# Three early quads of a fused attention and SiLU kernel take an M2 tile in 64-row halves

## The chip, the cores and the metric

The kernel runs on one core of a Trainium2 chip. The core has a matrix engine (TensorE, PE in the profile, whose weight loads are listed apart as PEld), three engines for elementwise work (VectorE or DVE, ScalarE or ACT, GpSimd or POOL), a queue engine (SyncE or SP) and 16 DMA engines. The metric is the device time of one execution in microseconds (us); lower is better.

## The reference

Per batch and head: scores, a causal mask with a decay from the cumulative sum of log f, softmax, times V. The result, laid out as 4608 tokens by 512, goes through two matrix products with a SiLU between them.

```
scores = scale * q @ k^T + (cum[i] - cum[j]),  -1e9 above the diagonal   # B=8, H=8, S=576, D=64
attn   = softmax(scores) ;  x = (attn @ v) as [4608, 512]
h = x @ w_in            # [512, 2048]
g = h * sigmoid(h)
out = g @ w_out         # [2048, 512]
```

## The kernel before

**Attention.** The decay is folded into V: V is multiplied by exp(-cum) on POOL (`convert_v`, L420), a column of ones in V gives the softmax denominator, and no maximum is subtracted. The first 128 query rows of all batches are done ahead of the main loop (the functions whose names end in 0). The main loop treats the other 448 rows. Heads go in pairs `n` (32 of them, four for each batch); two pairs are one *quad* `m` (16 of them). For a pair, `scores(n, c)` with c = 0, 1, 2 runs the score matmuls in three chunks (L470). Their contraction is over 64, so they are given to one half of the array's rows each ("64*128" in the profile), the two heads of a pair on the two halves at once. ACT takes the exponential (L481, and L475 for the 64 last rows). `mask` and `mask_tail` (L487, L493, DVE) clear what lies above the diagonal. `attend(n)` (L517, L526) multiplies with V on the full array, and DVE divides by the denominator (L534, L535) into `xr`. `back(m)` turns the quad's `xr` into columns of x: by seven PE transposes and two DVE copies (L559, L562, L565) for m = 0, 1, 2 and 15, by two DMA transposes on SP (L549, L553) for the others (`BY_DMA`).

**The two products.** x is held in 13 groups of 512, 384 or 256 tokens. *M1* is x @ w_in: `m1_chunk(g, fc)` makes one of 16 chunks of a group with four full-array matmuls (L578), a tanh on ACT (L586) and one DVE operation that completes twice the SiLU into `gt` (L587). *M2* is g @ w_out: a tile of 128 tokens is 16 full-array matmuls over 512 columns (L623), issued in four parts, and an ACT copy with the factor 0.5 (L633). A second form of M2, `m2_rows` (L640), does a tile with 64 matmuls over 64 rows and 256 columns (L649), two at a time on the two halves of the array, in two halves of 32 matmuls; it writes two PSUM tiles `pr` in place of one `po`. Between its halves DVE reads one column (`m2_fence`, L660), and `m2_out` (L662) evicts with two DVE operations (L666). PSUM is split in two score buffers (`psc`) and four others (`pbig`), which `hp`, `po`, `pr`, `tx` and `dn` share.

**What sets the order.** All five engines run in the order in which the program is written; nothing is reordered. `wanted` (L690) says whether M1 or M2 is next, `step` issues one chunk or part, `fill` and `slot` issue as many as fit in a number of microseconds at the planned rate, and `rest` goes on until the quad has its share (`QUAD`, L929). `whole` (L914) finishes an M2 tile that has been begun and a group whose M1 has at most four chunks left; it returns the next M2 tile, or nothing if there is none that may be started. `store` (L599) puts output DMAs on SP. `turn(n)` (L889) issues the work for later pairs: the cast of pair n+3 on POOL, the loads of pair n+4 on SP and POOL, a batch's V loads and conversions, and the DMA transpose of pair n+3 on SP (L438).

**The main loop** (L961) has two forms of a quad. Quads 0 to 3, without rows, run three bursts of scores with M1 and M2 between them on the full array: burst, `back`, slot, burst, slot, burst, slot, both `attend`, slot. Quads 4 to 15 start with `whole`, and if it gives a tile they run burst, first half of the M2 tile in 64-row form, burst, second half, burst, and put M1 and M2 chunks behind the first and the second `attend`. Here are the lines that choose:

```
rows = whole() if m > 0 and BY_DMA[m - 1] else None
scores(n, 0)
scores(n, 1)
if m > 0:
    back(m - 1)
```

Of the kernel before, what the change touches and what calls it, by code (L numbers as in the profile page):

```python
# [18 lines left out]
def kernel(  # L19
# [130 lines left out]
    def head(p, i):  # L150
        return p // 2 * 4 + 2 * i + p % 2
# [347 lines left out]
    BY_DMA = [3 <= m < NQ - 1 for m in range(NQ)]  # L499

    def attend(n):
        b, p = divmod(n, NP)
        if p % 2 == 0:
            xqs[n // 2] = xqp.tile([P, NGR, 2, D], BF16, name="xr", tag="xr", bufs=3)
        xq = xqs[n // 2]
        u, ut = us.pop(n), uts[n % 4]
        dn = pbig.tile([P, NGR, D + 1], FP32, name="dn", tag="big")

        def vals(kb, i):
            h = head(p, i)  # L510
            return v0[b][:, h, :] if kb == 0 else vbf[b][:, kb - 1, h, :]

        for i in range(2):
            for c in range(1, NM):
                for kb in range(c + 1):
                    o = AT[c, kb]
                    nc.tensor.matmul(  # L517
                        dn[:, i * NR + c - 1, :],
                        lhsT=u[:, i, o : o + P],
                        rhs=vals(kb, i),  # L520
                        start=(kb == 0),
                        stop=(kb == c),
                    )
        for i in range(2):
            for kb in range(NM + 1):
                nc.tensor.matmul(  # L526
                    dn[:, NGR - 1, :],
                    lhsT=ut[:, kb, i : i + 2, :].rearrange("p i t -> p (i t)"),
                    rhs=vals(kb, i),
                    start=(i == 0 and kb == 0),  # L530
                    stop=(i == 1 and kb == NM),
                )
        rec = recp.tile([P, NGR], FP32, name="rec", tag="rec")
        nc.vector.reciprocal(out=rec[:, :], in_=dn[:, :, D])  # L534
        nc.vector.tensor_tensor(  # L535
            out=xq[:, :, p % 2, :],
            in0=dn[:, :, 0:D],
            in1=rec[:, :, None].to_broadcast([P, NGR, D]),
            op=ALU.mult,
        )  # L540
# [58 lines left out]
    def store(n):  # L599
        n = max(n, 0)  # L600
        for q_, dst, src in stores[:n]:
            q_.dma_start(out=dst, in_=src)
        del stores[:n]
# [79 lines left out]
    at = {"m1": 0, "m2": 0, "left": 0.0}  # L683
# [23 lines left out]
    def step(force=0):  # L707

        a, c = at["m1"], at["m2"]
        want = wanted(a, c)  # L710
        if not want:
            return None
        g1 = M1[a][0] if a < len(M1) else NG
        g2 = M2[c][0] if c < len(M2) else NG
        can1 = g1 in ready and not (M1[a][1] == 0 and g1 > g2 + lag["g"])
        can2 = open2["w"] and c < len(M2) and g2 < g1
        kind = force if (force == 1 and can1) or (force == 2 and can2) else want
        if kind == 1:
            if M1[a][1] == 0:
                begin[g1] = (0, c)  # L720
            m1_chunk(g1, M1[a][1])
            at["m1"] += 1
            t = 4 * (GW[g1] / 2.4 + 2.5)
        else:
            m2_part(*M2[c])
            at["m2"] += 1
            t = 4 * (DM / 2.4 + 2.5)
        return t

    def behind():  # L730
        t = sum(4 * (GW[g] / 2.4 + 2.5) for g, _ in M1[at["m1"] :] if g in ready)
        t += sum(4 * (DM / 2.4 + 2.5) for g, _, _ in M2[at["m2"] :] if g in ready)
        return t / 1000
# [180 lines left out]
    def whole():  # L914

        while at["m2"] < len(M2) and M2[at["m2"]][2] and wanted(at["m1"], at["m2"]):
            t = step(2)
            at["left"] -= t / 1000
        c = at["m2"]
        while M1[at["m1"]][0] in ready and M1[at["m1"]][1] >= NFC - 4 and M2[c][0] == M1[at["m1"]][0]:  # L920
            at["left"] -= step(1) / 1000
        a = at["m1"]
        if c >= len(M2) or M2[c][2]:
            return None
        g1 = M1[a][0] if a < len(M1) else NG
        return M2[c][:2] if M2[c][0] < g1 else None

    LAG, LOW = 13.0, 2.0
    QUAD = [10.9] * (NQ // 2) + [11.7] * (NQ // 2)  # L929

    def spent():
        t = sum(4 * (GW[g] / 2.4 + 2.5) for g, _ in M1[: at["m1"]])
        return (t + at["m2"] * 4 * (DM / 2.4 + 2.5)) / 1000
# [15 lines left out]
    def passed():  # L949
        for x in pending:  # L950
            x[0] -= 1
        while pending and pending[0][0] == 0:
            ready.update(pending.pop(0)[1])

    def slot(us_, least=0, ends=(0, 0)):
        n = len(stores)
        fill(us_, least, ends)
        store(n)
        passed()

    for m in range(NQ):  # L961
        n = 2 * m
        piece = 1.7 if m < 2 else 2.4
        if m == 2:
            assert at["m2"] >= M2_OF[0]
            first_pool.__exit__(None, None, None)
            gpools[0] = ctx.enter_context(tc.tile_pool(name="third", bufs=1))
            lag["g"] = 2
        if m == 4:
            lag["parts"] = 12  # L970
        goal = (spent() if m <= 4 else goal) + QUAD[m]
        rows = whole() if m > 0 and BY_DMA[m - 1] else None
        scores(n, 0)
        scores(n, 1)
        if m > 0:
            back(m - 1)
        turn(n)
        if m > 0:
            if m % 2 == 0:
                b = m // 2 - 1  # L980
                pending.append([2, [REST_OF[b]] + ([TAILS_OF[b][0]] if b == NM - 1 else [])])
        if rows:
            at["m2"] += 4
            m2_rows(*rows, 0)
            m2_fence(*rows)
            mask(n)
            scores(n, 2)
            scores(n + 1, 0)
            turn(n + 1)
            m2_rows(*rows, 1)  # L990
            mask_tail(n)
            mask(n + 1)
            scores(n + 1, 1)
            scores(n + 1, 2)
            m2_out(*rows)
            passed()
            attend(n)
            mask_tail(n + 1)
            slot(1.9, 3)
            attend(n + 1)  # L1000
            slot(1.8)
            rest(goal)
            at["left"] = 0.0
            continue
        slot(piece, 0, (1, 0))
        mask(n)
        scores(n, 2)
        scores(n + 1, 0)
        turn(n + 1)
        slot(piece, 0, (1, 0))  # L1010
        mask_tail(n)
        mask(n + 1)
        scores(n + 1, 1)
        scores(n + 1, 2)
        mask_tail(n + 1)
        slot(piece, 0, (1, 0))
        attend(n)
        attend(n + 1)
        slot(min(3.5, max(0.8, behind() - LAG)) if m > 1 else 0.8)
# [40 lines left out]
```

## Time and profile before

| what | value |
|---|---|
| time, median of 3 runs | 340.76 us (340.21 to 341.42) |
| the profiled execution | 340.02 us, of which the span is 338.2 us |
| PE busy | 328.6 us, 97% |
| ACT, DVE, POOL busy | 216.7, 191.4, 157.8 us |
| M1 matmuls (L578) | 122.5 us in 700 records |
| M2 matmuls (L623, L649) | 89.8 us and 46.0 us |
| score matmuls (L470) | 27.8 us and more for the part against `kT` |

The profile shows one execution. Each line of a timeline starts with the start time and the duration in us; "x8" says that eight instructions are merged, and a bracket gives the idle time before them and what ended it. Matmuls overlap, so the step from the start of one group to the start of the next is the time that PE spent on it. A few matmul records are missing, so a group can show x3 where four ran. Times of a quad below run from its first score matmul to that of the next.

### The profile page before, as it was taken

What the parts mean: (1) busy time and instruction counts of PE and PEld (TensorE: products, weight loads), DVE (VectorE), ACT (ScalarE), POOL (GpSimd) and SP (SyncE); (2) the same over time, 40 slices, a digit from 0 to 9 for tenths busy, and PEclk for the clock granted to TensorE, in tenths of its full rate; (3) what the DMA queues carried; (4) which work ended last, traced back from release to release, by engine and by line L of the source; (5) the groups of instructions that cost most, each with busy time, mean ns of one, the idle gap of its engine ahead of it and who ended that gap; (6) DMA issues with size and microseconds to landing.
All of it is one profiled execution on the core that took longest, in us unless ns stands there. A gap on an engine that the chain in (4) does not pass through costs nothing.

```text
span 338.2 us, 9998 instructions
## 1 busy us (share of the span) xinstructions
PE 328.6 (97%) x4101; PEld 222.4 (66%) x4132; DVE 191.4 (57%) x425; ACT 216.7 (64%) x389; POOL 157.8 (47%) x241
## 2 busy tenths in 40 slices
PE   8999999999999999999999999999999999999995
PEld 3745655577656767858767796867777685555654
DVE  4667736276567456655655865785485565334330
ACT  5757645776777676848748794875778583444431
POOL 8895417637885675493493656819060000000000
PEclk9999999999999999999999999999999999999998
DMA  8999999999999999999999979969673200101012
GB/s 152 196 196 220 167 200 168 200 238 171 183 227 176 136 189 147 187 185 155 168 181 144 175 126 194 186 104 184 119 129 64 60 33 20 44 33 64 31 64 62
DMA packets 124542, 48.00 MB, mean 142 GB/s; under 512 B 111824, under 2 KB 118224, under 8 KB 124496
## 3 DMA queue, kind: packets, MB, share of 16 engines
q1 hardware_dynamic: 93200, 31.10, 51.1%
q0 software_dynamic: 31136, 16.13, 37.1%
q8 instruction: 32, 0.52, 0.7%
q10 hardware_dynamic: 160, 0.13, 0.1%
q14 instruction: 14, 0.11, 0.1%
HBM read 36.85 MB, written 9.44 MB: 137 GB/s over the span
## 4 chain that ended last, share of the span: by engine, by line
PE 87%; DMA 6%; POOL 3%; issue 1%; ACT 1%; DVE 0%; POOLq 0%
PE hp L578 33%; PE po L623 24%; PE pr L649 12%; PE sc L470 7%; PE dn L517 6%; DMA vf<-in_v_dram 5%; PE dn L526 3%; DMA qkb<-in_k_dram 1%; POOL v L350 1%; PE tp L295 1%; POOL qkb L132 1%; PE tx L559 1%; POOL w_in_bf L200 0%; ACT u L481 0%; ACT osb L633 0%
## 5 line engine op out<-in xcount | busy, mean ns | idle before, releaser
L587 DVE SCALAR_TENSOR_TENSOR gt<-th,hp 128x384 bf16<-128x384 bf16 (+2 forms) x208 | 107.2, 523 | 71.1 <-ACT th L586 62.7
L586 ACT ACTIVATE th<-hp 128x384 bf16<-128x384 f32 (+2 forms) x208 | 96.6, 471 | 73.8 <-PE hp L578 71.9
L578 PE MATMUL hp<-x,w_in_bf 128*128 128x384 bf16 (+2 forms) x700 | 122.5, 321 | 0.4
L578 PEld LDWEIGHTS <-w_in_bf 128*128 128x128 bf16 x832 | 78.9, 98 | 48.9 <-issue 0.5
L623 PE MATMUL po<-w_out_bf,gt 128*128 128x512 bf16 (+1 forms) x374 | 89.8, 370 | 1.7 <-issue 0.6
L481 ACT ACTIVATE u<-sc 128x1024 bf16<-128x1024 f32 (+1 forms) x96 | 74.7, 819 | 7.0 <-PE sc L470 7.0
L623 PEld LDWEIGHTS <-gt 128*128 128x128 bf16 x400 | 37.6, 98 | 32.5 <-issue 0.2
L411 POOL CAST qkb<-qf 128x384 bf16<-128x384 f32 x32 | 16.6, 520 | 74.6 <-DMA qf<-in_q_dram 74.0
L649 PE MATMUL pr<-w_out_bf,gt 64*128 64x256 bf16 x768 | 46.0, 269 | 0.0
L158 POOL DMA_DIRECT2D qkb<-in_k_dram x56 | 43.7, 782 | 0.6 <-issue 0.6
L649 PEld LDWEIGHTS <-gt 64*128 64x128 bf16 x768 | 38.6, 94 | 2.8
L424 POOL TENSOR_TENSOR vp<-vf,w_bf 128x520 bf16<-128x520 f32 (+1 forms) x32 | 34.3, 1075 | 9.2 <-DMA vf<-in_v_dram 7.5
L633 ACT ACTIVATE osb<-po 128x512 f32<-128x512 f32 (+1 forms) x25 | 14.6, 584 | 26.4 <-PE po L623 26.4
L470 PE MATMUL sc<-qkT 64*128 64x128 bf16 (+1 forms) x640 | 27.8, 206 | 0.3 <-ACT u L481 0.3
L487 DVE TENSOR_TENSOR u<-u,tri 128x768 bf16<-128x768 bf16 x32 | 20.6, 645 | 10.5 <-ACT u L481 10.5
L470 PEld LDWEIGHTS <-qkT 64*128 64x128 bf16 x640 | 20.0, 94 | 8.2 <-issue 6.5
L475 ACT ACTIVATE ut<-sc 128x640 bf16<-128x640 f32 x32 | 22.7, 709 | 1.9 <-PE sc L470 1.7
L517 PEld LDWEIGHTS <-u 128*128 128x128 bf16 x576 | 20.7, 98 | 3.4 <-issue 0.5
L517 PE MATMUL dn<-vp,u 128*128 128x65 bf16 x384 | 22.0, 194 | 0.4 <-issue 0.4
L535 DVE TENSOR_TENSOR xr<-dn,rec 128x448 bf16<-128x448 f32 x32 | 20.0, 624 | 1.1
L189 POOL DMA_DIRECT2D vf<-in_v_dram x24 | 20.2, 859 | 0.0
L517 PE MATMUL dn<-v,u 128*128 128x65 bf16 x192 | 20.0, 194 | 0.0
(73 smaller groups left out, 243.3 us busy)
## 6 DMA issues: line engine op xcount, KB each, us to landing
out_dram<-osb SPq DMA_DIRECT2D x32, 256.0 KB, 3.2
vf<-in_v_dram POOLq DMA_DIRECT2D x24, 256.0 KB, 6.1
qf<-in_q_dram SPq DMA_DIRECT2D x64, 96.0 KB, 3.6
qkb<-in_k_dram POOLq DMA_DIRECT2D x56, 48.0 KB, 3.9
vf<-in_v_dram SPq DMA_DIRECT2D x8, 256.0 KB, 5.3
w_in_bf<-in_moe_w_in_dram POOLq DMA_DIRECT2D x4, 512.0 KB, 7.1
w_out_bf<-in_moe_w_out_dram POOLq DMA_DIRECT2D x4, 512.0 KB, 9.2
qkb<-in_q_dram POOLq DMA_DIRECT2D x8, 128.0 KB, 5.4
```

The lines of the kernel that those rows point to most:

```text
L158: nc.gpsimd.dma_start(out=t2[:, NR + 1 : NX, j * D : (j + 1) * D], in_=k[b, head(p, j), P:SM, :].rearrange("(c p) d -> p c d", p=P),)
L424: nc.gpsimd.tensor_tensor(out=vbf[b][r, c, :, :], in0=vst[b][c][r, :, :], in1=w_bf[r, c + 1, b * H : (b + 1) * H, None].to_broadcast([n, H ...
L470: nc.tensor.matmul(sc[:, i, o : o + q1 - q0], lhsT=kt, rhs=t[r, q0:q1], start=True, stop=True)
L475: nc.scalar.activation(out=ut[:, :, 0:3:2, :].rearrange("p k i t -> p i k t"), in_=sc[:, :, T0 : T0 + (NM + 1) * ST].rearrange("p i (k t) ...
L481: nc.scalar.activation(out=u[:, :, c * SM : c * SM + w], in_=sc[:, :, 0:w], func=ACT.Exp, scale=scale)
L487: nc.vector.tensor_tensor(out=x, in0=x, in1=tri[:, None, None, :].to_broadcast([P, 2, NR, P]), op=ALU.mult)
L517: nc.tensor.matmul(dn[:, i * NR + c - 1, :], lhsT=u[:, i, o : o + P], rhs=vals(kb, i), start=(kb == 0), stop=(kb == c),)
L578: nc.tensor.matmul(hp[:, :], lhsT=w_in_bf[:, cc, fc * P : (fc + 1) * P], rhs=xcols(g, cc), start=(cc == 0), stop=(cc == NCC - 1),)
L586: nc.scalar.activation(out=th[:, :], in_=hp[:, :], func=ACT.Tanh, scale=0.5)
L587: nc.vector.scalar_tensor_tensor(out=gt[:, fc, :], in0=th[:, :], scalar=1.0, in1=hp[:, :], op0=ALU.add, op1=ALU.mult,)
L623: nc.tensor.matmul(po[:, :], lhsT=gt[:, fc, tb * P : (tb + 1) * P], rhs=w_out_bf[:, fc, m0:m1], start=(fc == 0), stop=(fc == NFC - 1),)
L649: nc.tensor.matmul(pos[g, tb][y], lhsT=gt[r, fc, tb * P : (tb + 1) * P], rhs=w_out_bf[r, fc, y * DM // 2 : (y + 1) * DM // 2], start=(half ...
```

## The change

`whole` is now called ahead of every quad, so a quad of the first four takes the 64-row form too if there is a tile to start. A new function `ones(k)` issues k chunks of M1. In the first four quads all stores that are due are issued at the head of the quad. Where `back(m - 1)` is made by PE transposes in a quad with rows, it moves behind the three score bursts and the first `attend` (`late`).

```
+    def ones(k):
+        n = len(stores)
+        for _ in range(k):
+            step(1)
+        at["left"] = 0.0
+        store(n)
+        passed()
...
-        rows = whole() if m > 0 and BY_DMA[m - 1] else None
+        rows = whole()
+        late = bool(rows) and m > 0 and not BY_DMA[m - 1]
+        if m < 4:
+            store(len(stores))
         scores(n, 0)
         scores(n, 1)
-        if m > 0:
+        if m > 0 and not late:
             back(m - 1)
         turn(n)
...
             attend(n)
             mask_tail(n + 1)
-            slot(1.9, 3)
+            if late:
+                back(m - 1)
+            if m < 2:
+                ones(4)
+            else:
+                slot(1.9, 3)
             attend(n + 1)
+            if m < 4:
+                if m < 2:
+                    ones(2)
+                else:
+                    slot(min(5.3, max(0.8, behind() - LAG)))
+                continue
             slot(1.8)
             rest(goal)
```

The order that comes out, M1 and M2 chunks by quad (a unit is one chunk of M1 or one part of M2; g is the group, tb the tile):

| quad | before | after |
|---|---|---|
| 0 | M2 g1 tb0 parts 0-2, M1 g2 chunks 0-5, among the bursts | M2 g1 tb0 whole, in rows; M1 g2 chunks 0-3, then 4-5 |
| 1 | M2 g1 tb0 part 3, tb1 parts 0-2; M1 g2 chunks 6-12 | M2 g1 tb1 whole, in rows; M1 g2 chunks 6-9, then 10-11 |
| 2 | M2 g1 tb1 part 3, g2 tb0, g2 tb1 part 0; M1 g2 chunks 13-15, g3 chunks 0-5 | M1 g2 chunks 12-15 first; M2 g2 tb0 whole, in rows; M2 g2 tb1 parts 0-2; M1 g3 chunks 0-4 |
| 3 | M2 g2 tb1 parts 1-3; M1 g3 chunks 6-13 | M2 g2 tb1 part 3 first; no rows, as no M2 tile may be started; M1 g3 chunks 5-6, 7-10, 11-14 between the bursts and 15 at the end |
| 4 | M1 g3 chunks 14-15 first; rows from here on | rows from here on |

The whole work is the same. PE has 64 matmuls in place of 16 for three M2 tiles, ACT three copies fewer, DVE six evictions and three fences more. From quad 4 on the two orders differ by one or two units. In the changed kernel an M2 part stands right ahead of the first scores of quads 14 and 15, as it does in quads 5, 7 and 9 of both.

## The prediction

> **What bounds the kernel now.** I read the page first, then who waited for the score matmuls, then PE's timeline through two kinds of quad, then the busy time in stretches cut at the quads.
>
> ```profile
> span 338.2 us, 9998 instructions
> ...
> PE 87%; DMA 6%; POOL 3%; issue 1%; ACT 1%; DVE 0%; POOLq 0%
> ```
>
> PE is 87% of the chain that ended last, so a change is worth what it takes from PE's own time or from PE's waits. A view of the score line says what ended PE's idle time ahead of it:
>
> ```profile
>   issue: 7.6, 24
>   ACT u L481: 0.3, 1
> ```
>
> 24 gaps end in "issue": the engine waited for nothing recorded. 24 is also 3 bursts in each of quads 0 to 3 and one in each of the other 12: the places where full-array work gives way to 64-row work. PE's timeline, here in quad 2 and quad 4, gives their price:
>
> ```profile
> 83.73 1.04 PE L578 MATMUL hp<-x,w_in_bf 128*128 128x256 bf16 x8
> 84.70 0.23 PE L470 MATMUL sc<-qkT 64*128 64x128 bf16 x2
> ...
> 109.92 1.91 PE L649 MATMUL pr<-w_out_bf,gt 64*128 64x256 bf16 x32
> 111.67 0.22 PE L470 MATMUL sc<-qkT 64*128 64x128 bf16 x2
> ```
>
> M1 runs at 0.437 us a chunk of 256 columns (four matmuls of 0.109, the step between chunks that follow one another), 0.650 a chunk of 384; an M2 part takes 0.863. Two chunks need 0.87 from 83.73, to 84.60; scores start at 84.70. A crossing costs 0.10, and the way back the same. A half tile in rows takes 111.67 - 109.92 = 1.75, with no gap on either side; two are 3.50 against 3.45 for the four parts.
>
> In stretches cut at the quads' first scores (columns: length, then busy time and instructions of PE, PEld, DVE, ACT, POOL, then clock and DMA):
>
> ```profile
> 61.94:71.33 9.39, 8.92 (x140) 6.29 (x142) 4.66 (x13) 7.52 (x14) 6.93 (x11) 1.00 1.17 245
> 71.33:81.92 10.59, 10.33 (x153) 7.38 (x156) 7.68 (x20) 8.44 (x18) 6.23 (x9) 1.00 1.47 173
> 81.92:96.36 14.44, 14.34 (x170) 8.89 (x173) 7.68 (x19) 9.68 (x18) 11.89 (x16) 1.00 1.15 174
> 96.36:109.47 13.11, 12.95 (x164) 8.11 (x165) 8.78 (x21) 10.48 (x19) 8.61 (x13) 1.00 1.27 218
> 109.47:123.64 14.17, 14.06 (x207) 10.13 (x209) 7.96 (x19) 9.06 (x15) 10.82 (x17) 1.00 1.01 172
> 137.62:152.46 14.84, 14.74 (x211) 10.51 (x213) 8.51 (x20) 9.55 (x16) 10.38 (x15) 1.00 1.30 193
> 152.46:165.21 12.75, 12.73 (x207) 9.76 (x206) 8.25 (x20) 10.05 (x17) 7.02 (x11) 1.00 1.40 174
> ```
>
> These are quads 0 to 4, 6 and 7. The clock is full throughout. I take M1 and M2 at the rates above off each length; what remains is attention, crossings and waits. Quad 0: 3 parts and 6 chunks are 5.21, rest 4.18. Quad 1: 6.51, rest 4.08. Quad 2: 10.39, rest 4.05. Quad 3 with the two chunks ahead of quad 4: 9.09, rest 4.02. Quads 4, 6 and 7 in rows: 10.80, 11.45 and 9.30, rest 3.37, 3.39 and 3.45. ACT has most of the rest of a quad: 10.48 of 13.11 in quad 3.
>
> **The change, part by part.** I sum against the profiled execution, 340.02 us (span 338.2 and 1.8 around it); the median, 340.76, stands 0.74 above it.
>
> *Quads 0 to 2 go to rows.* Crossings: three bursts with two each become one with two, so 4 x 0.105 = 0.42 a quad less, and 0.05 more for the slower tile. The quads show less than that, since scores in rows come closer to ACT: quads 4, 6 and 7 rest at 3.40 on average without `back`, and the seven transposes of `back` step 0.39 on PE (82.47 to 82.87 with its gap, 0.40). A quad with rows and late transposes is thus 3.79. Quad 1: 4.08 to 3.79, -0.29. Quad 2: 4.05 to 3.79, -0.26. Quad 0 has no `back` and has a wait of some 0.4 for ACT today (its second burst steps 0.96 where others step 0.53); it goes from 4.18 to 3.45 (quad 7, which also has an M2 copy on ACT ahead of it): -0.73. Sum: **-1.28**.
>
> The Trainium skill, page "TensorEngine Tiling (Array Packing)", section "Tiling Modes", says that changing the mode drains the engine, which agrees with the gaps of 0.10; the page "TensorE: Matmul & The Clock Gate", section "Single matmul latency", has some 166 ns for a matmul's latency beyond its columns, and with that as the price 12 crossings would be 2.0 us, an estimate from the page, where the rows give 1.26. The same tiling page, "PSUM Bottleneck", speaks against this change: faster matmuls leave PSUM's eviction as it was; if the two evictions of 0.415 us in each of three tiles stood on the path they would cost 2.5 us, but quads 4 to 7 rest lower with them than quads 1 to 3 without.
>
> *Chunks in a run behind `attend`.* Quads 0 and 1 now put four M1 chunks in a row between the two `attend`. Four chunks fill the four PSUM buffers; the second `dn` waits for the first chunk's tanh and DVE operation, which stand behind the last exponentials. No row shows four chunks of 256 there. Quads 5 and 7 run three of 384 in that place with nothing to quad 7's sum (zero end); quad 5 has a pause of 0.6 there (other end, once in each quad, 1.2; below zero nothing, as the chunks can't run faster). Tanh and eviction of one 256-column chunk are 0.38 and 0.42, PE needs 1.75 for the four: nearly covered. The late copies (0.56 and 0.22 on DVE) stand ahead of these evictions in quad 1. I take **+0.25**.
>
> *Quad 3 keeps the old form but has more M1.* It had 3 M2 parts and 8 chunks; now one part ahead and 11 chunks of 384, ten of them among the bursts. The copy of M2 goes ahead of its exponentials as well. Steps of ACT, from starts of neighbours:
>
> ```profile
> 84.66 0.68 ACT L586 ACTIVATE th<-hp 128x256 bf16<-128x256 f32 x2
> 85.19 0.75 ACT L475 ACTIVATE ut<-sc 128x640 bf16<-128x640 f32 x1
> 85.77 1.36 ACT L481 ACTIVATE u<-sc 128x256 bf16<-128x256 f32 x2
> 86.94 0.47 ACT L586 ACTIVATE th<-hp 128x256 bf16<-128x256 f32 x1
> ```
>
> So an `ut` steps 0.58, the short and the long exponential together 1.17 (0.26 and 0.91). A tanh of 384 lasts 0.49; I let it step 0.39, as neighbours overlap by 0.1. From the first score of quad 3: the copy ends at 0.6, two exponentials 2.43, chunks 5 and 6 3.21, tail and short exponential 4.05, long one 4.97, chunks 7 to 10 6.53, then exponential, tail and short one 8.29, chunk 11 done at 8.78. PE: transposes and two chunks to 2.24, burst, four chunks 2.88 to 5.48, burst, four chunks 6.1 to 8.7. Then `attend(6)` needs a PSUM buffer, and the oldest is that of chunk 11: its DVE operation lasts 0.55 and ends at about 9.4. PE waits **+0.7**. Ends: 0 (quad 3 of before, whose mix has no such wait) and 1.3 (the second `attend` delayed by as much again, less the overlap).
>
> *Late quads.* An M2 part stands ahead of quads 14 and 15; quad 5's second burst steps 0.61 where quad 4's steps 0.50, for the copy on ACT. Two such: **+0.2** (0 to 0.3).
>
> *Stores at the head, and the queues.* In quad 0 four stores pass the loads of pair 4 and the transpose of pair 3 on SP; they took 66.93 to 69.3, 2.4 us. The transpose went out at 65.58 and lands within some 5 us (4.5 median); 2.4 later is 72.5, and its scores run at about 74. The store of quad 0's tile now passes the loads of pair 6, the tails and batch 1's V, 0.5 more. POOL's own order stays; its casts follow these loads. PE's cover is the three pairs of lead; price **0**, and the rival below says what if it is not. The other stores of the four quads move by less. ACT loses three copies, DVE gains three tiles' evictions and fences, 0.99 us each; DVE is busy 7.7 of 10.6 us at most in quads 0 to 2, so they cost nothing while it keeps ahead of PE.
>
> *Everything after* is PE in the same amount. Sum: -1.28 + 0.25 + 0.7 + 0.2 = -0.13 on 340.02; on the median 340.6. The quad-3 and PSUM terms lean on my slowest readings, so I say 340.5.
>
> **Rivals.**
>
> *A: quad 3 and the PSUM buffers hold, faster.* ACT's 10.1 us of steps in quad 3 fit in PE's 11.2, so the wait may be 0.1. Then -1.28 + 0.1 + 0 + 0.1 = -1.08: 339.7. For it: PE shows one wait for ACT in the whole main loop (0.3). Against: in quad 3 the order, not the sum, makes the wait.
>
> *B: batch 1's V comes late, slower.* `attend(4)`, the first of batch 1, comes nearer, since quad 2 puts nothing on PE between the bursts but the tile.
>
> ```profile
> 66.93 2.36 SPq L602 DMA_DIRECT2D out_dram<-osb  x4
> 85.34 2.38 POOL L424 TENSOR_TENSOR vp<-vf,w_bf 128x520 bf16<-128x520 f32 x2 [1.68 <-DMA vf<-in_v_dram]
> 91.07 0.19 PE L517 MATMUL dn<-v,u 128*128 128x65 bf16 x1
> ```
>
> V is ready at 87.7 and used from 91.07. In the new order quad 2's `attend` starts at about 61.94 + 9.5 + 9.8 + 1.75 (four chunks ahead) + 5.1 (scores and tile) = 88.1 and reads the last block 0.65 later, at 88.8: 1.1 of slack. The 2.9 us of stores put ahead of pair 4's load and of V would, if passed on whole, make V ready at 90.6 and PE wait 1.8: -0.13 + 1.8, 342.4. It decides from about 2.3 us of delay, where the total crosses 1 us. Against: the same four stores stood ahead of these loads before too, only pair 4's load and pair 3's transpose are newly behind; I expect 0.5 to 1 us.
>
> *C: the halves do nothing.* If ACT, not crossings, set the pace of a rows quad, quads 0 to 2 would rest as before, -0.4 from quad 0's wait alone; with quad 3, +0.75: 341.5. Against: 3.40 in quads 4, 6, 7.
>
> **How the numbers follow.** My forecast 0.46, A 0.25, B 0.16, C 0.13. A difference of 0.3% (1.02 us) is about what a measurement of this kernel can tell from no change. A's centre lies just beyond it, and goes to faster for the most part with a little of the forecast: 0.25. B and part of C, with the forecast's tail: 0.23 slower. Within 0.3%: 0.52. Range 339.3 (A with no wait at all, -1.28 with some gain in quad 1) to 342.2 (most of B); the forecast's own range is 339.8 to 341.4.
>
> **What would show it.** Right: gaps ended by "issue" ahead of scores fall from 24 to 18; quads 0 to 2 rest at about 3.5, 3.9 and 3.8; quad 3 rests at 4.7, with PE idle ahead of its first `attend` behind a DVE operation on `gt`; quad 4 starts about 0.3 us sooner than at 109.47; work after it keeps its length. Wrong: a wait of `dn` for POOL `vp` in quad 2, a rest of 4 in quads 0 to 2, or quad 3 at 4.0.

## The result and the profile after

The changed kernel takes 343.28 us (median of 16 runs, 341.73 to 345.13); the kernel before took 340.95 us (16 runs, 339.12 to 343.98). The ratio is 1.0074, with a 95% interval of 1.0053 to 1.0096: the change made the kernel slower by 0.74%, some 2.5 us. Ratios here and below leave out the few runs that lie over 1.5% above the fastest of their kernel. The profiled execution of the changed kernel took 342.15 us, of which the span is 340.4 us, against 340.02 and 338.2 before.

The page and PE's waits in the changed kernel (engine and line, what it waited for, us in total, times, longest):

```profile
span 340.4 us, 10319 instructions
...
PE 84%; DMA 7%; POOL 3%; ACT 2%; issue 2%; DVE 2%; POOLq 0%; DVEq 0%; ACTq 0%
```

```profile
PE hp L578 <- DVE osb L666: 1.8, 1, 1.8
PE wm L242 <- DVE warm L214: 1.2, 1, 1.2
PE dn L526 <- issue: 1.2, 1, 1.2
PE dn L517 <- DVE gt L587: 0.5, 1, 0.5
```

Three of these are new or grown: a wait for an output eviction, a pause for nothing recorded (0.4 us before), and a wait for a chunk's `gt`. The stretches tell which quads they are in (columns as before: length, busy time and instructions of PE, PEld, DVE, ACT, POOL, then clock and DMA):

```profile
61.43:73.11 11.68, 9.83 (x193) 8.48 (x192) 6.23 (x16) 7.97 (x14) 6.01 (x9) 1.00 1.19 225
73.11:84.77 11.66, 11.66 (x216) 10.42 (x216) 8.39 (x24) 9.52 (x19) 7.17 (x12) 1.00 1.32 167
84.77:98.64 13.87, 13.87 (x212) 10.11 (x213) 8.64 (x21) 8.57 (x15) 11.74 (x17) 1.00 1.28 178
98.64:110.54 11.90, 11.37 (x156) 7.36 (x157) 8.40 (x21) 9.88 (x19) 8.01 (x12) 1.00 1.19 213
...
126.04:141.25 15.21, 14.02 (x239) 11.01 (x240) 8.53 (x20) 11.33 (x19) 8.67 (x12) 1.00 1.36 175
```

These are quads 0 to 3 and 5. PE is busy to the last in quads 1 and 2 and has idle time in 0, 3 and 5. With M1 and M2 taken off as in the prediction (0.437 or 0.650 us a chunk, 0.863 a part), this *rest* stands so:

| quad | before | forecast | after |
|---|---|---|---|
| 0 | 4.18 | 3.45, and 0.13 for the run of chunks | 5.61 |
| 1 | 4.08 | 3.79, and 0.12 for the run of chunks | 3.84 |
| 2 | 4.05 | 3.79 | 3.71 |
| 3 | 4.02 | 4.7 | 4.75 |
| 5 | 4.02 | 4.02 | 4.77 |
| 14 | 3.34 | 3.44 | 3.50 |

The quads not listed agree within 0.03 us. The sum of the differences is 1.43 - 0.24 - 0.34 + 0.73 + 0.03 + 0.75 + 0.16, and 0.11 behind the start of quad 15; the loop starts 0.51 earlier (61.43 for 61.94, which nothing in the change explains: among the other kernels here with the same order ahead of the loop it lies between 61.7 and 62.6). Together 2.1 of the 2.2 us by which the span grew.

**Quad 0.** The chain of what ended last, and the timelines of SP and DVE, show the wait:

```profile
64.03 0.70 ACT ut L475
64.74 0.04 ACT u L481
64.78 4.38 DMA out_dram<-osb
69.15 0.03 issue
69.18 0.02 DVEq L666
69.20 0.05 issue
69.25 0.76 DVE osb L666 x2
```

```profile
61.78 1.55 SPq L438 DMA_TRANSPOSE qkT<-qkb  x1
63.38 0.62 SPq L177 DMA_DIRECT2D qktf<-in_q_dram  x1
64.04 0.64 SPq L177 DMA_DIRECT2D qktf<-in_k_dram  x1
64.78 2.29 SPq L602 DMA_DIRECT2D out_dram<-osb  x4
```

```profile
69.25 0.76 DVE L666 TENSOR_SCALAR osb<-pr 128x256 f32<-128x256 f32 x2 [2.73 <-DMA out_dram<-osb]
69.92 0.19 DVE L534 RECIPROCAL rec<-dn 128x7 f32<-128x7 f32 x1
70.15 0.62 DVE L535 TENSOR_TENSOR xr<-dn,rec 128x448 bf16<-128x448 f32 x1
70.69 0.21 DVE L493 TENSOR_TENSOR ut<-ut,trit 128x128 bf16<-128x128 bf16 x1
70.82 1.49 DVE L587 SCALAR_TENSOR_TENSOR gt<-th,hp 128x256 bf16<-128x256 bf16 x4
```

The pool of output tiles `osb` has four buffers (`opool`, L64). The four tiles of group 0 hold them when the loop begins. Their stores stand at the head of quad 0 in the program, but on SP behind a transpose and the loads of the tails, and the first leaves at 64.78 and lands 4.38 us later. The tile in rows is now finished within quad 0, so the fifth `osb` is wanted at about 66.5. Before, this fifth tile was finished only in quad 1. DVE, which evicts it now, stands still for 2.73 us, and all that is queued behind it on DVE is late with it: the two operations of `attend(0)`, a mask, four chunks. Two of the four PSUM buffers still hold the tile's two `pr`. PE fills the other two, with `attend(0)` and one chunk, and then waits 1.8 us for one of the two that the eviction would free.

**Quad 5.** PE's timeline in the changed kernel, and in the kernel before:

```profile
131.71 0.25 PE L526 MATMUL dn<-vp,ut 128*128 128x65 bf16 x3
133.13 0.19 PE L526 MATMUL dn<-vp,ut 128*128 128x65 bf16 x1 [1.17 <-issue]
133.16 0.19 PE L526 MATMUL dn<-v,ut 128*128 128x65 bf16 x1
```

```profile
131.68 0.19 PE L517 MATMUL dn<-v,u 128*128 128x65 bf16 x1
132.28 0.27 PE L517 MATMUL dn<-vp,u 128*128 128x65 bf16 x3 [0.41 <-issue]
```

The pause is in the middle of an accumulation, whose operands were all used by matmuls just before: neither data nor a buffer is missing. It was there before, at 0.41 us, and is now 1.17 and at another matmul. The experiments below take it up.

**What came as forecast.** The gaps ahead of the score matmuls fall from 24 (7.6 us) to 18:

```profile
  issue: 5.8, 17
  DMA qf<-in_q_dram: 0.3, 1
```

The eighteenth is put down to a DMA that the matmul does not need. In quad 3 PE waits 0.53 us ahead of `attend(6)` for a chunk's DVE operation.

### The profile page after: what moved, and what is told of

The parts are those of the page before. It is cut to its first block, busy times and chain, and to the rows that moved or that the text cites. A ratio compares the mean times of both kernels' runs of the same rounds, so it can differ in the third digit from the quotient of the medians.

```text
span 340.4 us, 10319 instructions
## 1 busy us (share of the span) xinstructions
PE 330.5 (97%) x4276; PEld 228.2 (67%) x4276; DVE 192.9 (57%) x434; ACT 216.5 (64%) x386; POOL 158.1 (46%) x241
## 4 chain that ended last, share of the span: by engine, by line
PE 84%; DMA 7%; POOL 3%; ACT 2%; issue 2%; DVE 2%; POOLq 0%; DVEq 0%; ACTq 0%
PE hp L578 31%; PE po L623 21%; PE pr L649 15%; PE sc L470 6%; PE dn L517 5%; DMA vf<-in_v_dram 5%; PE dn L526 3%; DMA qkb<-in_k_dram 1%; DMA out_dram<-osb 1%; DVE gt L587 1%; POOL v L350 1%; PE tp L295 1%; POOL qkb L132 1%; ACT th L586 1%; POOL w_in_bf L200 0%
## 5 line engine op out<-in xcount | busy, mean ns | idle before, releaser
L623 PE MATMUL po<-w_out_bf,gt 128*128 128x512 bf16 (+1 forms) x352 | 81.1, 369 | 0.0
L649 PE MATMUL pr<-w_out_bf,gt 64*128 64x256 bf16 x960 | 57.5, 269 | 0.0
L623 PEld LDWEIGHTS <-gt 128*128 128x128 bf16 x352 | 33.6, 98 | 29.2
L411 POOL CAST qkb<-qf 128x384 bf16<-128x384 f32 x32 | 17.6, 550 | 73.8 <-DMA qf<-in_q_dram 73.2
L649 PEld LDWEIGHTS <-gt 64*128 64x128 bf16 x960 | 48.2, 94 | 3.5
L633 ACT ACTIVATE osb<-po 128x512 f32<-128x512 f32 (+1 forms) x22 | 12.7, 578 | 27.2 <-PE po L623 24.2
L487 DVE TENSOR_TENSOR u<-u,tri 128x768 bf16<-128x768 bf16 x32 | 19.3, 603 | 13.2 <-ACT u L481 13.2
```

The costliest lines, as they stand in the source:

```text
L623: nc.tensor.matmul(po[:, :], lhsT=gt[:, fc, tb * P : (tb + 1) * P], rhs=w_out_bf[:, fc, m0:m1], start=(fc == 0), stop=(fc == NFC - 1),)
L649: nc.tensor.matmul(pos[g, tb][y], lhsT=gt[r, fc, tb * P : (tb + 1) * P], rhs=w_out_bf[r, fc, y * DM // 2 : (y + 1) * DM // 2], start=(half ...
```

## The experiments

Theory one: the output buffer costs quad 0 some 2.1 us, and quad 3's mix of work 0.7. Rival: DVE is late in quad 0 for its own added work. Theory two came later, from the traces: PE pauses in quad 5 because its instructions come late. All runs at a glance; *rest* as above, times in us. Each ratio is to the kernel before as measured together with that run, with medians of 340.95 to 341.67 us, so ratios compare better than medians:

| run | median | ratio to before (95%) | rest of quads 0, 1, 2, 3, 5 |
|---|---|---|---|
| after | 343.28 | 1.0074 (1.0053 to 1.0096) | 5.61, 3.84, 3.71, 4.75, 4.77 |
| early1 | 349.99 | 1.0246 (1.0218 to 1.0275) | 3.45, 4.75, 3.71, 4.87, 4.19 |
| noq0 | 344.92 | 1.0097 (1.0064 to 1.0130) | 4.18, 3.99, 6.55, 4.76, 5.07 |
| quad3 | 341.46 | 0.9992 (0.9964 to 1.0020) | 7.37, 3.84, 3.68, 4.10, 3.44 |
| early1_quad3 | 348.81 | 1.0209 (1.0173 to 1.0244) | 3.45, 4.04, 3.68, 4.12, 3.72 |
| first | 342.61 | 1.0049 (1.0017 to 1.0082) | 3.44, 3.84, 4.59, 4.75, 7.29 |
| first_quad3 | 340.21 | 0.9988 (0.9959 to 1.0016) | 3.44, 3.84, 4.26, 4.09, 4.04 |
| first_quad3_behind | 340.29 | 0.9970 (0.9937 to 1.0004) | 3.44, 3.93, 3.68, 4.09, 3.44 |
| headstores | 341.23 | 1.0011 (0.9975 to 1.0047) | 4.18, 4.08, 4.41, 4.02, 3.92 |
| five | 342.66 | 1.0048 (1.0012 to 1.0083) | 3.44, 4.00, 5.04, 4.75, 6.40 |
| five_quad3 | 341.76 | 0.9997 (0.9964 to 1.0031) | 3.44, 3.84, 4.42, 4.09, 3.44 |
| clean_turns_back | 340.60 | 0.9968 (0.9932 to 1.0005) | 3.44, 3.85, 3.86, 4.09, 7.62 |
| after_pad | 343.04 | 1.0049 (1.0013 to 1.0084) | 3.44, 3.84, 3.71, 4.75, 3.44 (quad 7: 5.20) |
| before_pad32 | 339.94 | 0.9964 (0.9939 to 0.9990) | 4.18, 4.08, 4.05, 4.02, 3.44 |
| after_pad224 | 345.83 | 1.0132 (1.0093 to 1.0170) | 3.44, 3.84, 5.83, 4.75, 4.89 |
| five_pad224 | 346.15 | 1.0141 (1.0096 to 1.0187) | 3.44, 3.84, 6.29, 4.75, 5.05 |
| best_pad224 | 343.63 | 1.0072 (1.0038 to 1.0105) | 3.50, 3.84, 4.71, 4.09, 4.26 |

### Quad 0: whose wait is it?

**early1**: the first tile is stored from ACT's queue, right behind its eviction.

```
+            if g == 0 and tb < 1:
+                nc.scalar.dma_start(out=out[tb * S : tb * S + P, :], in_=osb[:, :])
+                return
```

> The changed kernel, but the first M2 tile's output (group 0, tile 0) is stored from ScalarE's queue right behind its eviction, so that one of the four output buffers is free long before quad 0 needs a fifth. Buffer theory: the eviction of quad 0's tile in rows no longer waits for a store, the rest of quad 0 falls from 5.6 to between 3.5 and 3.8 us, the kernel gains about 1.9 us over the changed one and stands 0.3 to 0.6 us (0.1 to 0.2%) above before. PSUM rival (four M1 chunks in a run fill the buffers behind a late tanh): quad 0 rests at 5 us or more, ratio to before stays near 1.007. DMA rival (the moved stores crowd the loads): quad 0 a little better, but waits in quads 2 to 5 remain, ratio 1.005 or more.

Quad 0 rests at 3.45 and the eviction's wait is gone. But the kernel is far slower, ahead of the loop, which begins at 70.55 in place of 61.43:

```profile
ACT th L586 <- DMA kf<-in_k_dram: 8.9, 1, 8.9
```

A tanh needs no K load. The trace has the store and a K load of SP on the same completion counter: the load lands at 52.77, and ACT issues the store at 52.85, and the tanh behind it. So the edit shows the wait, and its time says nothing of what removing it brings.

**noq0**: quad 0 keeps the old form.

```
-        rows = whole()
+        rows = whole() if m > 0 else None
```

> The changed kernel with quad 0 left in the old form (its stores still issued at the head); rows from quad 1 on. Buffer theory: by quad 1 the stores have landed, so no eviction waits; quad 0 rests near 4.2 us, quads 1 and 2 near 3.8, quad 3 near 4.7; against before +0.7 - 0.5 and so +0.2 us, ratio 1.000 to 1.003. PSUM rival: quad 1 has the same run of four chunks and would show a wait of about 2 us in place of quad 0. DMA rival: ratio stays at 1.005 or more.

Quad 0 is back at 4.18 with no wait, and the kernel is slower still, where 1.000 to 1.003 was expected. Quad 2 now rests at 6.55, for the second of these lines; the first holds two pauses like that of quad 5 above, 1.45 us in quad 5 and 1.09 in quad 7:

```profile
PE hp L578 <- issue: 2.5, 2, 1.5
PE sc L470 <- DMA qkT<-qkb: 2.2, 1, 2.2
```

Pair 5's transpose, behind the stores that were put at the head, comes 2.2 us too late for its scores. In the changed kernel quad 0's own delay had covered for that. This is the prediction's rival B in its place (quad 2) and by its cause (stores ahead of loads), on `qkT` where it had named V.

**first**: SP issues the first store ahead of the loads for pair 3 and the work that follows from them.

```
-    load_qk(3)
-    cast_qk(2)
-    transposes(2)
-    load_tails(1)
-    for c in range(NM):
-        convert_v(0, c)
...
     fill(6.0)
+    store(len(stores))
+    load_qk(3)
+    cast_qk(2)
+    transposes(2)
+    load_tails(1)
+    for c in range(NM):
+        convert_v(0, c)
     two_more(6)
```

> The changed kernel, but SyncE issues one store, that of the first M2 tile, ahead of the loads and the transpose of the last pairs before the loop (it is the same queue, so no semaphore of another queue is in the way); the other three stay at the head of quad 0. Buffer theory: the store lands some 4 us sooner than quad 0's tile needs its buffer, DVE does not wait, quad 0 rests at 3.5 to 3.8 us in place of 5.6, quad 3 still at 4.7; the kernel falls by 1.5 to 2 us against the changed one, ratio to before 1.000 to 1.003. Late-load rival: with quad 0's wait gone, quads 1 and 2 come to their scores and their V sooner than the loads that the stores passed, so that a part of it, 1 to 2 us, comes back as a wait of PE for a DMA transpose or for POOL in quad 2, ratio 1.004 to 1.008.

Quad 0 rests at 3.44, which is the forecast's own 3.45. Quad 2 gives 0.5 us back to `qkT`, and quad 5 has a pause of 2.0.

**five**: a fifth output buffer, and no store or load moved. The room is taken from K's staging.

```
-    opool = ctx.enter_context(tc.tile_pool(name="opool", bufs=4))
+    opool = ctx.enter_context(tc.tile_pool(name="opool", bufs=5))
...
-            t = stage.tile([P, NR, 2, D], FP32, name=name, tag=name, bufs=3)
+            t = stage.tile([P, NR, 2, D], FP32, name=name, tag=name, bufs=3 if name == "qf" else 2)
```

> The changed kernel with five output buffers in place of four; the room comes from the staging of K, two buffers in place of three, and in the trace of the changed kernel no K load would have waited for that (the third K load leaves SP at 50.98 us, the first K cast ended by 49.5). No store and no load moves. Theory (output buffer): DVE no longer waits for a store to land in quad 0, PE's wait at hp of 1.8 us goes, quad 0 rests at 3.4 to 3.6 in place of 5.61. Rival (DVE is late there for its own work, or for something else): quad 0 stays above 4.5. What quad 0 held back now comes two microseconds early: pair 5's transpose stands behind the stores, so quad 2 may wait for qkT, 4.2 (as with the first store ahead of the loads, 4.59) and at worst 6.5 (as without rows in quad 0). Quad 3 4.75, quad 5 4.0 to 7. Time: 343.3 - 2.1 + 0.5 + 0 to 1 = 341.7 to 342.7.

Quad 0 rests at 3.44 with all DVE work in place. So it is the buffer: DVE's own added work costs nothing there, and the rival falls. Part of the gain goes to quad 2 (5.04, where a burst waits 0.8 us) and to a pause of 2.80 in quad 5:

```profile
134.39 0.19 PE L526 MATMUL dn<-vp,ut 128*128 128x65 bf16 x1 [2.80 <-issue]
```

In timed runs, *first* and *five* are 0.25% below *after*, less than the two intervals can tell apart.

### Quad 3, and the order behind it

**quad3**: quad 2 gives up two units and quad 3 does not call `whole`, so that quad 3 has nearly its old share (11 chunks and 2 parts for 10 and 3) and the order from quad 4 on is that of before.

```
-        rows = whole()
+        rows = whole() if m != 3 else None
...
+            elif m == 2:
+                slot(0.8, 1)
             else:
                 slot(1.9, 3)
```

> The changed kernel with quad 3's mix put back: quad 2 issues one M2 part behind its first attend instead of three, and quad 3 does not finish the begun tile ahead of its scores, so it has M2 parts and fewer M1 chunks among its bursts, and the order from quad 4 on is that of before. Theory of quad 3's mix: its rest falls from 4.75 to 4.0 to 4.1 us, PE no longer waits for DVE ahead of attend(6), the whole stands 0.7 us under the changed kernel (ratio to before 1.004 to 1.006). If that wait came from elsewhere, quad 3 keeps 4.7. Quad 0 keeps its wait for an output buffer, rest 5.6 (buffer theory).

Quad 3 rests at 4.10 in place of 4.75, quad 5 at 3.44 in place of 4.77, and the time falls by 0.82% of before, some 2.8 us where 0.7 was expected. Quad 0 shows what a wait can grow to. The same wait is 3.25 us for DVE here and 2.3 for PE, and then PE's clock is halved (the column ahead of the last two):

```profile
DVE osb L666 <- DMA out_dram<-osb: 3.2, 1, 3.2
```

```profile
70.90:74.30 3.40, 3.09 (x23) 2.30 (x23) 2.58 (x8) 1.11 (x3) 0.38 (x1) 0.50 1.15 234
```

Quad 0 rests at 7.37: 2.3 for the wait, some 1.6 more at half clock.

The same edit on three other versions: **early1_quad3**, **first_quad3** and **five_quad3** are *early1*, *first* and *five* with it.

> Both edits at once. If the two waits are all that made the change slower, quads 0 to 3 rest at about 3.6, 3.8, 3.7 and 4.1 us, 15.2 against 16.3 before, and the kernel is 1.0 to 1.3 us faster than before, ratio 0.996 to 0.997. DMA rival: at best equal to before, ratio 1.000 to 1.004, with waits for loads, V or the DMA transposes.

> The same store moved, and quad 3's mix as in the run quad3. Two-waits theory: quads 0 to 3 rest at 3.6, 3.8, 3.7 and 4.1 us, 1.0 to 1.2 us less than before, ratio 0.996 to 0.998. Late-load rival: a wait for a load in quad 2 takes it back, ratio 0.999 to 1.004.

> Five output buffers, and quad 3's own M1 load put back as before (quad 2 gives up two units, so that the order from quad 4 on is that of before). Theory: quad 0 3.45, quad 1 3.84, quad 2 3.7 to 4.3, quad 3 4.10, quad 5 3.4 to 4.0; the rests of quads 0 to 5 sum to 22.3 against 23.7 before, so 1.0 to 1.4 us faster than before less a wait of up to 0.6 in quad 2: ratio 0.996 to 0.9985. Rival (the rows form brings nothing in the whole, its gain is eaten by later waits): ratio 0.9995 to 1.001.

Quad 3 rests at 4.09 to 4.12 in all of them. Against the version without the edit, the time falls by 0.37%, 0.61% and 0.51% of before. Four pairs point the same way, 1.3 to 2.8 us, and the traces show only 0.65 of it in quad 3 and 0.27 behind quad 13. In the traces quad 5 has most of the rest: 0.8, 3.9 and 3.0 us above its usual 3.44 in the three versions without the edit, and 0.3, 0.6 and 0.0 with it. One trace each does not show that the timed runs split so. And *five_quad3*, whose first six quads rest 1.1 us below those of before in its trace, is timed at 0.9997: outside what the theory gave (0.996 to 0.9985) and inside what the rival gave (0.9995 to 1.001). *first_quad3*, at 0.9988, also came out above its 0.996 to 0.998. The intervals, 0.3% each way, hold both readings.

### The stores

**headstores**: the kernel before with nothing but the stores at the head of the first four quads.

```
+        if m < 4:
+            store(len(stores))
```

> The kernel before with nothing but the stores moved to the head of the first four quads. My prediction and the buffer theory: no change, ratio 0.998 to 1.002, quads 0 to 3 rest at 4.0 to 4.2 as before. Late-load rival: slower by 1 us or more (1.003 and up), with a wait of PE for a DMA transpose or of attend(4) for V.

Of quads 0 to 3 only quad 2 moves, by 0.36, with a wait of 0.2 for `qkT`; the time is 1.0011 with an interval that holds 1. By itself the early issue costs little.

**first_quad3_behind**: *first_quad3*, with quad 0's other stores behind the loads of pair 4 and the transpose of pair 3, where they were before.

```
-        if m < 4:
+        if 0 < m < 4:
             store(len(stores))
...
         turn(n)
+        if m == 0:
+            store(len(stores))
```

> As first_quad3, but the other three stores of quad 0 stand behind the loads of pair 4 and the transpose of pair 3 again, where before has them. If stores ahead of the loads cost nothing, this equals first_quad3 within 0.3%. Late-load rival: it is 0.5 to 2 us faster than first_quad3, and no scores wait for a DMA transpose in quad 2; ratio to before 0.995 to 0.998.

No load is waited for any more, and the first six quads rest at 21.9 in place of the 23.7 of before (the first 15 at 52.3 for 54.1). Its profiled span is 336.1 us, the lowest of all. Timed it is 0.997, with an interval that just reaches 1.

**clean_turns_back** is that version with `back` in its old place among the bursts of quads 1 and 2.

```
-        if m > 0 and not late:
+        if m > 0:
             back(m - 1)
...
-            if late:
-                back(m - 1)
```

> The version with the first store ahead of the loads, the other three behind the turn of pair 3, and quad 3 in the old mix, but with back(m - 1) in its old place, between the second and the third burst, in quads 1 and 2. Theory (two crossings of 0.10 more, transposes and copies among the bursts): quads 1 and 2 rest 0.2 longer each, 4.1 and 3.9 in place of 3.93 and 3.68, time 0.3 to 0.5 us above 340.3. Rival (the late copies in DVE's queue, ahead of the evictions behind attend, cost as much as the crossings): same within 0.1 in both quads.

Quad 2 rests 0.18 longer, quad 1 0.08 shorter (against the 3.84 that other runs have, it is even). So the move of `back` is worth 0.1 us a quad on average, near the two crossings of 0.10 in one quad and nothing in the other. The timed runs cannot tell the two apart.

### Quad 5: PE's instructions

The trace's DMA records hold a queue that brings instructions; the page of the changed kernel has its sum (packets, MB, share):

```profile
q8 instruction: 33, 0.54, 0.7%
```

Each packet is 16 KB, and PE alone has about 8500 instructions (a weight load and a matmul for each step): 33 packets are one for every 256 of them, with 64 bytes each. Counted over PE's recorded instructions from the start of the program, every such pause lies at the same place in the count of 256 (at instruction 193 or 194 of it; this place is called the border here), and PE goes on 2.7 to 3.2 us after a packet has started (3.5 in *first_quad3*). Mostly the packet starts within 2 us of PE's crossing the border before (395 of 489 from quad 0 on, in all 18 kernels); behind the first border in quad 5 it starts 2.3 to 5.7 us after (once 1.5). So the pause should be that delay, and 2.8, less the time in which PE uses up the block:

| run | delay | PE's time for the block | delay + 2.8 - time | pause measured |
|---|---|---|---|---|
| before, quad 5 | 4.5 | 6.7 | 0.6 | 0.41 |
| after, quad 5 | 4.1 | 5.6 | 1.3 | 1.17 |
| first, quad 5 | 4.6 | 5.6 | 1.8 | 2.0 |
| five, quad 5 | 5.7 | 5.6 | 2.9 | 2.80 |
| clean_turns_back, quad 5 | 5.4 | 5.6 | 2.6 | 2.39 |
| after_pad, quad 7 | 5.7 | 6.8 | 1.7 | 1.60 |
| after_pad224, quad 5 | 5.3 | 6.5 | 1.6 | 1.29 |
| quad3, quad 5 | 3.1 | 5.6 | 0.3 | none |
| before_pad32, quad 5 | 3.1 | 5.6 | 0.3 | none |
| first_quad3_behind, quad 5 | 2.8 | 5.6 | 0.0 | none |

These are ten of the cases. Eight other pauses of over 0.1 us lie at such borders. For six of them the sum comes within 0.2 us, with PE's time taken between the borders less the pause (*noq0* 1.45 and 1.09, *five_pad224* 1.45, *best_pad224* 0.65, *early1* 0.59, *headstores* 0.30). It gives none for the 0.44 in *first_quad3* and the 0.12 in *early1_quad3*. In the other blocks of the 489 it gives no more than the 0.3 of the table, and no pause is there.

The changed kernel has 304 PE instructions more ahead of quad 5 (288 for the three tiles, 16 for two units that now stand earlier), one block and 48. That puts a block of quad 5 where PE is through it in 5.6 us (64-row matmuls and `attend`, the shortest block of this kernel) in place of 6.7.

**after_pad** moves the borders by 128 instructions and is meant to move nothing else.

```
-    keep_warm(10)
+    keep_warm(2)
+    t = pbig.tile([P, SM], FP32, name="wm", tag="big")
+    for _ in range(72):
+        nc.tensor.matmul(t[:, 0:P], lhsT=warm[:, 0:P], rhs=warm[:, 0:P], start=True, stop=True)
```

> The changed kernel with 72 warm-up matmuls of 128 columns in place of 8 of 512 in the first 6 us: the same time there, 64 matmuls, that is 128 PE instructions, more ahead of everything else. Theory (PE's instruction fetch): the pause of quad 5 is tied to a border of 256 instructions, counted from the start of the program, so it leaves the first attend(10), where it was 1.17 us, for the place 128 instructions earlier, among the half tile's matmuls, where PE takes longer for 256 instructions: 0 to 0.6 left there; quad 5 rests at 3.4 to 4.0 in place of 4.77. Quads 0 to 3 as in the changed kernel (5.6, 3.8, 3.7, 4.75). Time 342.5 to 343.0. Rival (the pause belongs to attend(10), a buffer or data it needs): it stays at the same matmul at 1.2 us, quad 5 4.77, time 343.3.

The pause has left quad 5, which rests at 3.44; so it does not belong to `attend(10)`. (That quad 0 does not wait here is no reason for it: in *first* and *five* it does not wait either, and the pause stays at the same matmul.) A pause of 1.60 turns up at another border, in quad 7:

```profile
164.94 0.19 PE L520 MATMUL dn<-v,u 128*128 128x65 bf16 x1 [1.60 <-issue]
```

The padded matmuls cost 2.8 us at the start, which I had not allowed for, and the time, 343.04, holds that. Quad 0's wait is gone here too, though no store was moved: the loop begins 2.9 us later (64.32) and meets stores that SP had issued anyway.

**before_pad32, after_pad224, five_pad224, best_pad224** use smaller matmuls for it (17 of 16 columns for one of 512, or 122 for all ten). The first gives the kernel before, in quad 5, the borders of *quad3*, 16 instructions from those of the changed kernel; the others add 224 instructions, 32 short of a block, to the changed kernel, to *five* and to *first_quad3_behind*.

```
-    keep_warm(10)
+    keep_warm(9)
+    t = pbig.tile([P, SM], FP32, name="wm", tag="big")
+    for _ in range(17):
+        nc.tensor.matmul(t[0:D, 0:16], lhsT=warm[:, 0:D], rhs=warm[:, 0:16], start=True, stop=True)
```

> The kernel before with 17 warm-up matmuls of 16 columns in place of one of 512, 32 PE instructions more, nothing else moved. Fetch theory: a block of 256 instructions that PE used up in over 6.6 us everywhere in the main loop now falls so that one takes 5.6 us in quad 5 (from about 124 us); with a packet that starts 4 to 4.6 us after the border and the 2.9 us that PE needs after its start, PE stands still for 4.1 + 2.9 - 5.6 = 1.4 us there (up to 2.1): quad 5 rests at 4.7 to 5.5 in place of 4.02, the time grows by 0.7 to 2 us, ratio 1.002 to 1.006. Rival (order, not count): quad 5 4.02, ratio 1.000 plus or minus 0.001 (the head by 0.4 us at most).

> The changed kernel with 122 warm-up matmuls of 16 columns in place of 10 of 512: 224 PE instructions more. The head may grow by up to 2 us, which the start of the first scores against 61.43 tells and which is to be taken off. Fetch theory: no block in the main loop is used up in under 6.0 us; quad 5 rests at 3.4 to 3.9 in place of 4.77, time less the head's growth 343.3 - 0.9 to 2 = 341.3 to 342.4 (less again if the later start spares quad 0 its wait for the store, as it did with the other padding). Rival (order): quad 5 4.77 with the pause at the same matmul of attend(10), time less the head's growth 343.3.

> The version with five output buffers and the same padding. Fetch theory: quad 5 3.4 to 3.9 in place of 6.40, no pause of 2.8 us at the dn matmul; time less the head's growth 342.66 - 1 to 2.5 = 340.2 to 341.7. Rival: quad 5 above 4.7, 342.7 plus the head's growth.

> The version with the first store ahead of the loads, three stores behind the turn, and quad 3 in the old mix (340.29 us, ratio 0.997), with the same padding. Its profile had no pause, but its border lies at the place where others pause. Fetch theory: timed runs had some, so less the head's growth it is 0 to 1 us faster, ratio 0.994 to 0.997. Rival: 0.997 less nothing, plus the head's growth.

Here my expectations fell. *before_pad32* came out faster than before, 0.9964 with an interval that ends at 0.9990. Its block is the short one, but its packet was 3.1 us late and not 4.1, and quad 5 has no pause (3.44 for 4.02); all other quads agree with before within 0.02 us, and the head is 0.37 longer. The three with 224 began the loop 3.8 us later (65.22 for 61.43, 65.37 and 65.58), more than I had allowed for; that much less, they stand at 342.0, 342.3 and 339.9, within what their intervals can tell from 343.28, 342.66 and 340.29. No quad 5 of these three came down to the 3.4 to 3.9 expected of the first two. The pause stayed in quad 5 and went to the border's new place (1.29, 1.45 and 0.65 us; *first_quad3_behind* without the padding had none in its trace). The first of them:

```profile
138.79 0.48 PE L580 MATMUL hp<-x,w_in_bf 128*128 128x384 bf16 x2 [1.29 <-issue]
```

With quad 0's wait gone by the late start, *after_pad224* waits in quad 2 in its place, as *noq0* did:

```profile
PE sc L472 <- DMA qkT<-qkb: 1.8, 1, 1.8
```

What is shown: the pause sits at a border of 256 instructions, and its size follows from the packet's delay, with the two exceptions named. What is not: why the packet is late in quad 5, and how late it is in timed runs. Beside every late packet of the table SP has a transpose that takes 3.8 to 6.9 us in place of 1.25, so the DMA engines may be what both wait for; no run here separates them. Nor does the count of instructions alone decide: the delay was 1.5 to 5.4 us in seven kernels with the same border in quad 5. Nor does a short block: in the kernel before, quads 11 and 14 have blocks of 5.4 us, whose packets started 1.8 and 0.7 us ahead of the crossing, and no pause.

## Why the prediction was wrong

- **"Stores at the head, and the queues", price 0**, is the first step that failed, and the largest in the trace. It asked what the stores delay, and never which buffer they free. Its sentence that DVE's evictions "cost nothing while it keeps ahead of PE" was true of DVE's work (*five*: 3.44 with all of it) and left out that an eviction must have an `osb`. The row to read was there: the first store in the profile of before left at 66.93 for tiles of group 0, all four buffers were taken until then, and the change wanted a fifth tile in quad 0. In the trace the term is 2.16 us (5.61 for 3.45); what it is in a timed run is open (below).
- **"Quads 0 to 2 go to rows", -1.28**: right where nothing else is in the way. The rests were 3.84 and 3.71 for 3.79 in quads 1 and 2, and 3.44 for 3.45 in quad 0 as soon as a buffer was free. The gaps fell from 24 to 18.
- **"Chunks in a run behind `attend`", +0.25**: the zero end, 0.05 in quad 1 and none in quad 0.
- **"Quad 3 keeps the old form but has more M1", +0.7**: 0.73, with the wait at `attend(6)` that was named, 0.53. Rival A falls with it.
- **"Late quads", +0.2**: 0.27, of which 0.16 in quad 14.
- **Rival B** (stores ahead of loads make quad 2 wait) was hidden in the changed kernel by quad 0's delay. It showed as 0.3 to 2.3 us for `qkT` in seven versions in which quad 0 did not wait for a buffer (and 0.2 in *headstores*); a V that came late cost 0.2 to 0.4 at most. It was a term of the same step.
- **Rival C** falls by quads 1 and 2.
- **"Everything after is PE in the same amount"** is the second step that failed. It missed quad 5: 0.75 over before, 1.33 over a quad without a pause. It took the small pause of before (cited only as an end of another term) for part of the quad, and did not ask what it was.

With these the profiled spans add up. The timed ones do so less well. Taking the buffer's wait away moved the median by -0.25% (*first*, *five*) and by 0 with the old quad 3 (*five_quad3* against *quad3*), where the traces have 2 to 4 us less in quad 0 and 0.7 to 1.3 us of it back in quad 2; the intervals are some 0.3% each way. Putting quad 3 and the order behind it back moved it by 0.4 to 0.8% every time. The runs of a kernel that was timed ten times or more differ among themselves by 3 to 7 us, and a profile is one of them: *five_quad3* was profiled at 338.9 us (span 337.1), 2.9 below its median. So the places and mechanisms are shown in the traces, and the split of the 2.5 us among them in a timed run is not: there the old quad 3 and the order behind it brought more than the buffer did. Nor is it shown that rows in the early quads pay in the end: *first_quad3_behind*, which has the change without its two waits, is 0.997, and 32 idle instructions gave the kernel before 0.9964.

## What to carry to other kernels

When work is moved earlier, list for each instruction that comes sooner which buffer of a pool it needs and which transfer frees it: issue, queue and landing (here 4.4 us), not issue alone. When a wait is found, ask what it covers for; here most cures of quad 0 uncovered a wait in quad 2, mostly for a late transpose. And where differences of 0.3% are at stake, shift the instruction stream by some idle instructions in both kernels before a cause is looked for in the order.

## What the hardware showed that was not expected

- PE can run out of instructions: pauses of 0.4 to 2.8 us, at borders of 256, when a packet started 3 to 6 us late. The Trainium skill, page "Runtime: NRT & Kernel Launch", section "Instruction fetch mechanics", has the same blocks of 16 KiB and 256 instructions and calls the crossing "mostly hidden"; the table above is where it was not.
- 32 idle instructions at the start changed a kernel's time by -0.36% (0.10 to 0.61%), more than most edits here did.
- Some pauses of PE cost twice. After one of 2.3 us in *quad3*, 2.0 in *first* and 2.4 in *clean_turns_back* the clock was halved for 3.4 us, as this stretch of *first* has it; after 2.8 in *five* it was not. In all traces the stretches of full clock between two changes last a whole number of 3.41 us (19 and 78 of them in *quad3*, 37 and 60 in the other two). Cut into such pieces, a trace has 2.0 to 2.4 us of idle PE in the piece ahead of each of these three half clocks; the 2.8 of *five* fell on two pieces (1.6 and 1.2), and pieces with up to 1.8 us were not followed by one. The Trainium skill, page "TensorE: Matmul & The Clock Gate", section "Part 1: The HAM clock gate (the "warmup" mystery)", has half rate after an idle window of about 3.4 us that runs freely; shorter pauses were enough here.

```profile
132.90:136.40 3.50, 3.50 (x17) 1.81 (x17) 2.32 (x4) 0.93 (x2) 3.26 (x5) 0.51 1.02 144
```

- Every timed run has its mean granted clock on record, and it tells whether the run had such a half clock: 0.988 to 0.995 in the five profiled executions that have one in mid-span, 0.997 or more in the other 13. The changed kernel has 0.995 or less in 7 of 16 runs, the kernel before in 16 of the 108 whose clock is on record. In *five* and *first_quad3_behind* it is 8 of 22, and with 224 instructions of padding 0 of 14. This fits long pauses in timed runs too, which the padding shortens. It does not show them: a half clock does not name its pause, and *first_quad3* has none in 12 runs without padding.
- A store on another engine's queue can make that engine wait for a load that it has nothing to do with (8.9 us in *early1*, where the two share a completion counter).
